# Delta-rule attention with a gated MLP: a new chunk loop in the source's order, with one tile per kind for both sides and two matmul streams in opposite quadrants

## The chip, the core and the metric

The kernel runs on one core of a Trainium2 chip. The time is device time in microseconds (us) of one execution, lower is better. A profiled execution comes with a trace of every engine: PE (TensorE, matmuls), PEld (its weight loads), DVE (VectorE), ACT (ScalarE), POOL (GpSimd) and SP (SyncE, which here only issues DMAs). The span is the time from the first to the last instruction of the trace.

## The reference

Two parts follow each other. The first is a recurrence over 768 tokens for each of 32 heads (4 batches of 8 heads, head dimension 48), with normalized keys:

```python
for t in range(S):
    y[:, :, t] = einsum('bhd,bhde->bhe', q[:, :, t], state)
    v_old = einsum('bhde,bhd->bhe', state, kt)
    state = state + bt * einsum('bhd,bhe->bhde', kt, vt - v_old)
```

The heads' outputs are laid side by side to x, (4, 768, 384). The second part is a gated MLP: h = gelu(x @ w_in) with w_in (384, 1024); the left half of h is u, the right half is normalized over its 512 columns and mixed over the tokens by w_sg (768, 768), plus a bias for each token; the product with u goes through w_out (512, 384) and is added to x.

## The kernel before, in words

**Chunks.** The recurrence is cut into 12 chunks of 64 tokens (NCH = 12, T = 64). Within a chunk it becomes a small triangular system for each head. The 32 heads lie as two sides of 16: side 0 on partitions 0 to 63, side 1 on 64 to 127. Two chunks form a segment (NSEG = 6).

**Triangular part.** `gram` (L174) makes k·kT and k·qT of a chunk: one matmul for each head, 48 rows of contraction, 128 columns (k and q side by side in `kd`). ACT copies the k part to `g`, which goes to DRAM (`gd`); DVE or ACT with POOL masks the q part into `MQ`. `lanes_a` (L223) reads the diagonal 32x32 blocks of a whole segment back as `z`, 128 blocks on 128 partitions, and makes the norms. `lanes_b` (L265) inverts the blocks by elimination on DVE, 30 steps of up to four tensor operations (L282, L286). `zstore` (L295) takes the inverted blocks through DRAM to the two tiles `ZW` of each chunk, one for each side. `solve` (L325) forms the corner block between the two 32x32 blocks with 32x32 matmuls (`corner`, two steps) and then `keys`: key times inverse, into free rows of the same ZW tile.

**Chain.** `chain` (L379) is the part that goes from chunk to chunk: `update` (one matmul for a head over 112 or 128 rows, which hold the value rows and the state rows together), `state` (key times update, added into a bank of PSUM that is never cleared) and `read` (again 112 or 128 rows). `us` holds the scaled values (`vprep`, on POOL, L375) and the state side by side.

**MLP, first half.** `ffn` (L472) takes 128 rows of x for two batches: transposes, a split into a high and a low part for three-term matmuls (`mm3`, L464 to L466), the value half (512 columns) with gelu, moments and the normalization, and four gate blocks (256 columns). x, u and the normalized values go to DRAM. There are 12 such units. Ten are handed out as filling in the chunk loop, the last two follow after it.

**MLP, second half.** After the loop `spatial` and `project` do the token mixing and the last matmul for one batch after another.

**What sets the order.** The loop at L606 weaves lists of steps by their index, `weave` puts the ffn steps between them by a running balance `lack` (L71, L89), `bank` may add filler matmuls on a tile `busy` (L75), and on top of that the program is ordered by a planner that simulates the engines: an instruction is issued where the planner puts it, not where it stands in the source. Two points are fixed by hand (`issue_after`, L588). All large DMAs are issued by SP.

**Precision.** The small matmuls are float32: each one is two MATMUL instructions with a weight load each, so a step over 16 heads is 32 instructions in the trace when both sides go along with 8 heads.

Of the kernel before, what the change touches and what calls it, by code (L numbers as in the profile page):

```python
# [18 lines left out]
DM = NH * HD  # L19
# [14 lines left out]
DIM = (slice(64, 112), slice(0, 48))  # L34
ROWS = (slice(0, 112), slice(0, 128))

DUTY = 1.0
N_KICK = 20  # L40
N_WARM = 9
XB = 2
AHEAD = 500.0
GQ = lambda nc: nc.sync
CREDIT = 2000.0
STREAMS = ((0, 7), (7, 32))
N_SOFT = 6
# [3 lines left out]
def delta_rule_gmlp_kernel(  # L51
    ctx: ExitStack,
    tc: tile.TileContext,
    kqT: bass.AP,
    ktok: bass.AP,
# [9 lines left out]
    nc = tc.nc  # L65

# [4 lines left out]
    lack = [0.0]  # L71

    def keep_warm(ps, n, lhsT=None):
        for _ in range(n):
            nc.tensor.matmul(out=ps, lhsT=busy[:, 0:P] if lhsT is None else lhsT, rhs=busy, start=True, stop=True)  # L75

    def bank(most=0):
        ps = psum.tile([P, 512], F32, name="ps")
        while most > 0 and lack[0] > 0:
            keep_warm(ps, 1)  # L80
            lack[0] += DUTY * 216 - 512
            most -= 1
        return ps

    def mm(out, lhsT, rhs, start=True, stop=True):
        nc.tensor.matmul(out=out, lhsT=lhsT, rhs=rhs, start=start, stop=stop, skip_group_check=True)  # L86
        k, m = lhsT.shape
        n = math.prod(rhs.shape[1:])
        lack[0] += DUTY * (max(0.833 * m, 0.833 * n) + 5) - 2 * n * k / P  # L89
        lack[0] = max(lack[0], -CREDIT)  # L90

    busy = const.tile([P, 512], BF16, name="busy")
    nc.vector.memset(busy, 0.0)
    kick = const.tile([P, P], BF16, name="kick")
    nc.vector.memset(kick, 0.0)

    ident = const.tile([P, P], F32, name="ident")
    make_identity(nc, ident)
    beta_l = const.tile([P, NSEG, 32], F32, name="beta_l")
    nc.scalar.dma_start(out=beta_l, in_=beta)  # L100
    winh = const.tile([P, NC, DFF], F32R, name="winh")
    winl = const.tile([P, NC, DFF], F32R, name="winl")
    xD = [dram.tile([NT, P, DM], F32, name=f"xD{b}", bufs=1) for b in range(NB)]
    vD = [dram.tile([NT, P, DH], F32, name=f"vD{b}", bufs=1) for b in range(NB)]
    uD = [dram.tile([ND, P, SEQ], F32, name=f"uD{b}", bufs=1) for b in range(NB)]
# [8 lines left out]
    N_MQ, N_ZW, N_K, N_US, N_KD, N_G = 6, 3, 3, 2, 4, 5  # L114

    mask = prep.tile([P, T], F32, name="mask")
    nc.gpsimd.memset(mask, 1.0)
    for sd in range(2):
        nc.gpsimd.affine_select(
            out=mask[TOK[sd]], in_=mask[TOK[sd]], pattern=[[1, T]], base=0,  # L120
            channel_multiplier=-1, compare_op=ALU.is_gt, fill=0.0,
        )

    kd = [prep.tile([112, 2, NH, T], F32, name=f"kd{i}") for i in range(N_KD)]

    MQ = [[(low if i < 3 else main).tile([P, NP, T], F32, name=f"mq{sd}_{i}") for i in range(N_MQ)] for sd in range(2)]
    ZW = [[main.tile([P, NP, T], F32, name=f"zw{sd}_{i}") for i in range(N_ZW)] for sd in range(2)]
    US = [[main.tile([P, NP, HD], F32, name=f"us{sd}_{i}") for i in range(N_US)] for sd in range(2)]
    KT = [main.tile([P, NP, HD], F32, name=f"kt{i}") for i in range(N_K)]
    for i in range(N_MQ):  # L130
        nc.gpsimd.memset(MQ[1][i][32:64], 0.0)

    def clear_zw(i):
        nc.gpsimd.memset(ZW[0][i][32:64, :, 0:32], 0.0)
        nc.gpsimd.memset(ZW[1][i][96:128, :, 0:32], 0.0)
        nc.gpsimd.memset(ZW[1][i][32:64], 0.0)

    for i in range(N_ZW - 1):
        clear_zw(i)
    for i in range(N_US):  # L140
        nc.gpsimd.memset(US[1][i][32:64], 0.0)
    nc.gpsimd.memset(US[0][0][64:112], 0.0)
    nc.gpsimd.memset(US[1][0][0:48], 0.0)

    cb = [bank() for _ in range(NB)]
# [13 lines left out]
    G, kqs, gdt, ztile = {}, {}, {}, {}  # L159

    def load(c, hf):
        if c >= NCH:
            return
        kq = kd[(2 * c + hf) % N_KD]
        kqs[c, hf] = kq
        nc.sync.dma_start(out=kq, in_=kqT[c, :, :, hf * NH:hf * NH + NH])

    def qload(c):
        for sd in range(2):
            nc.sync.dma_start(out=MQ[sd][c % N_MQ][DIM[sd]], in_=kqT[c, 64 * sd:64 * sd + HD, 1])  # L170

    def gram(c):
        if c >= NCH:
            return []  # L174
        c2, mqi = c % 2, c % N_MQ
        if c2 == 0:
            gdt[c // 2] = dram.tile([2, 2, 2, NP, 32, 32], F32, name="gd")
        gd = gdt[c // 2]
        g = main.tile([P, NP, T], F32, name="g", bufs=N_G)
        G[c] = g  # L180

        def quad(qd):
            kq = kqs[c, qd // 2]
            ps = bank(3).rearrange("p (j x t) -> p j x t", x=2, t=T)
            for j4 in range(4):
                j = (4 * qd + j4) % NH
                for sd in range(2):
                    rows = slice(64 * sd, 64 * sd + HD)
                    mm(ps[TOK[sd], j4], kq[rows, 0, j], kq[rows, :, j])
                yield  # L190
            js = slice(4 * qd, 4 * qd + 4)
            nc.scalar.copy(out=g[:, js, :], in_=ps[:, :, 0, :])  # L192
            for sd in range(2):
                mq = MQ[sd][mqi][TOK[sd], js, :]
# [578 lines left out]
```

## Time and profile before

| | |
|---|---|
| median of 3 runs | 656.38 us (651.7 to 660.0) |
| the profiled execution | 651.14 us |
| its span | 649.4 us |
| mean granted TensorE clock | 0.841 |
| PE busy | 523.4 us, 81% |
| PEld busy | 454.4 us, 70% |
| DVE busy | 379.8 us, 58% |
| ACT busy | 255.6 us, 39% |
| POOL busy | 135.7 us, 21% |
| DMA queue of SP | 81.95 MB, 47% of the 16 engines' span |

Busy time of PE is the union of the modelled spans of its matmuls, which overlap each other; the rate of a stream of matmuls is read from the distance between starts. The granted clock is 0.50 or 1.00 at any moment; a figure between them is a mean over a stretch. DVE, ACT and POOL execute in the order of their queues, as does SP with its DMA issues: one that waits holds up those behind it.

### The profile page before, as it was taken

To read this page: it belongs to the slowest core of one execution; us is meant where nothing else is said; L and a number is where in the kernel's file an instruction comes from. 1 tells how busy PE (TensorE), PEld (TensorE's weight loads), DVE (VectorE), ACT (ScalarE), POOL (GpSimd) and SP (SyncE) were. 2 spreads that over 40 slices of the span, in tenths; PEclk is the share of its full clock that TensorE was granted. 3 is DMA by queue.
4 is the path that set the end of the run, shared out by engine and by line. 5 is a ranking of instruction groups with operands and counts; after the bars stand their busy time and mean duration, and the time that the engine had idled before them with its cause. 6 is when DMAs were issued, how large, how long until landed. Compare 5 with 4: busy or idle time off the path is not lost. (4 is left out here: it accounts for less than half of the span.)

```text
span 649.4 us, 16992 instructions
## 1 busy us (share of the span) xinstructions
PE 523.4 (81%) x6943; PEld 454.4 (70%) x6943; DVE 379.8 (58%) x1274; ACT 255.6 (39%) x581; POOL 135.7 (21%) x142
## 2 busy tenths in 40 slices
PE   7272794634588696975799979898899999999997
PEld 5251473624467484854678858786789999999997
DVE  3899799119823697349714795396467453533332
ACT  2140372613363454542455646457654121311100
POOL 8326561132001020010101011131001321222210
PEclk9655777557779598987779979599999999999999
DMA  9898540564246364650463334544598264431123
GB/s 205 219 228 190 131 141 26 117 160 126 79 90 156 90 189 126 151 141 25 133 146 100 108 99 132 118 138 125 152 304 262 78 203 122 144 106 51 49 74 111
DMA packets 114175, 86.81 MB, mean 134 GB/s; under 512 B 68272, under 2 KB 96560, under 8 KB 114096
## 3 DMA queue, kind: packets, MB, share of 16 engines
q1 hardware_dynamic: 108864, 81.95, 47.0%
q0 software_dynamic: 864, 3.15, 1.5%
q10 hardware_dynamic: 4368, 0.62, 0.6%
q8 instruction: 55, 0.90, 0.6%
q14 instruction: 24, 0.20, 0.1%
HBM read 56.85 MB, written 28.84 MB: 132 GB/s over the span
## 5 line engine op out<-in xcount | busy, mean ns | idle before, releaser
L375 POOL TENSOR_TENSOR us<-us,nv 64x768 f32<-64x768 f32 x24 | 38.7, 1617 | 233.7 <-DMA us<-vtok 125.5
L86 PE MATMUL ps<-kd 48*64 48x128 f32 x768 | 67.7, 333 | 23.2 <-DMA kd<-kqT 18.0
L282 DVE TENSOR_TENSOR ztmp<-z 128x119 f32<-128x119 f32 (+36 forms) x318 | 77.1, 274 | 1.2
L86 PEld LDWEIGHTS ps<-kd 48*64 48x64 f32 x768 | 55.2, 167 | 31.8 <-DMA kd<-kqT 19.9
L286 DVE TENSOR_TENSOR z<-z,ztmp 128x119 f32<-128x119 f32 (+36 forms) x318 | 73.5, 262 | 1.2
L701 POOL TENSOR_TENSOR ga<-ga,uT 128x384 f32<-128x384 f32 x32 | 33.8, 1055 | 153.8 <-ACT ut L534 51.8
L86 PE MATMUL ps<-us,mq 112*64 112x48 f32 (+1 forms) x768 | 40.1, 242 | 28.7 <-ACT zw L364 13.2
L86 PEld LDWEIGHTS ps<-us,mq 112*64 112x64 f32 (+1 forms) x768 | 36.1, 155 | 36.2 <-ACT zw L364 13.7
L545 ACT CAST gh<-ga 128x384 fp32r<-128x384 f32 x32 | 16.4, 514 | 102.7 <-POOL ga L701 102.6
L464 PE MATMUL ps<-winh,xh 128*128 128x512 f32 x72 | 38.6, 537 | 16.5 <-ACT xh L545 16.5
L202 DVE TENSOR_TENSOR mq<-ps,mask 64x256 f32<-64x256 f32 x64 | 27.0, 421 | 35.3 <-ACT g L192 27.7
L464 PE MATMUL ps<-xh,winh 128*128 128x256 f32 x144 | 42.4, 301 | 1.9 <-DVE mq L202 1.9
L465 PE MATMUL ps<-xl,winh 128*128 128x256 f32 x144 | 40.4, 282 | 0.0
L466 PE MATMUL ps<-xh,winl 128*128 128x256 f32 x144 | 40.3, 282 | 0.0
L546 DVE TENSOR_TENSOR gl<-ga,gh 128x384 fp32r<-128x384 f32 x32 | 17.8, 555 | 38.3 <-ACT gh L545 38.3
L364 ACT COPY zw<-ps 48x512 f32<-48x512 f32 x48 | 27.9, 581 | 27.4 <-PE ps L86 26.8
L86 PE MATMUL ps<-zw,kt 64*48 64x64 f32 x768 | 32.5, 242 | 6.8 <-DVE mq L202 6.4
L86 PE MATMUL ps<-us,zw 128*64 128x48 f32 (+1 forms) x768 | 36.4, 239 | 1.5 <-ACT zw L364 1.2
L466 PE MATMUL ps<-winh,xl 128*128 128x512 f32 x72 | 32.7, 454 | 5.1 <-DVE xl L546 5.1
L86 PEld LDWEIGHTS ps<-zw,kt 64*48 64x48 f32 x768 | 28.0, 139 | 11.9 <-issue 7.1
L86 PEld LDWEIGHTS ps<-us,zw 128*64 128x64 f32 (+1 forms) x768 | 31.7, 151 | 5.8 <-issue 3.6
L86 PEld LDWEIGHTS ps<-j,ztk 32*32 32x32 f32 x768 | 18.4, 127 | 24.8 <-ACT j L350 11.9
(139 smaller groups left out, 1280.4 us busy)
## 6 DMA issues: line engine op xcount, KB each, us to landing
kd<-kqT SPq DMA_DIRECT2D x24, 448.0 KB, 6.1
uD<-ut SPq DMA_DIRECT2D x24, 256.0 KB, 3.6
uT<-uD SPq DMA_DIRECT2D x8, 768.0 KB, 4.8
vD<-vg SPq DMA_DIRECT2D x20, 256.0 KB, 2.9
vraw<-vD SPq DMA_DIRECT2D x20, 256.0 KB, 4.2
us<-vtok SPq DMA_DIRECT2D x24, 192.0 KB, 3.8
kt<-ktok SPq DMA_DIRECT2D x12, 384.0 KB, 3.9
mq<-kqT SPq DMA_DIRECT2D x24, 192.0 KB, 7.5
```

The costliest lines, as they stand in the source:

```text
L86: nc.tensor.matmul(out=out, lhsT=lhsT, rhs=rhs, start=start, stop=stop, skip_group_check=True)
L202: nc.vector.tensor_tensor(out=mq, in0=ps[TOK[sd], :, 1, :], in1=mask[TOK[sd]].unsqueeze(1).broadcast_to([64, 4, T]), op=ALU.mult,)
L282: nc.vector.tensor_tensor(out=tv, in0=z[:, r0:r1, i:i + 1].broadcast_to([P, r1 - r0, w]), in1=z[:, i:i + 1, i + 1:32].broadcast_to([P, r1 ...
L286: nc.vector.tensor_tensor(out=z[:, r0:r1, i + 1:32], in0=z[:, r0:r1, i + 1:32], in1=tv, op=ALU.add)
L364: nc.scalar.copy(out=ZW[sd][zi][DIM[sd], js], in_=ps[DIM[sd]])
L375: nc.gpsimd.tensor_tensor(out=us[TOK[sd]], in0=us[TOK[sd]], in1=nvs[c // 2][TOK[sd], c % 2].unsqueeze(2).broadcast_to([64, NP, HD]), op=AL ...
L464: nc.tensor.matmul(out=ps, lhsT=sh, rhs=mh, start=(first and i == 0), stop=False)
L465: nc.tensor.matmul(out=ps, lhsT=sh, rhs=ml, start=False, stop=False)
L466: nc.tensor.matmul(out=ps, lhsT=sl, rhs=mh, start=False, stop=(last and i == n - 1))
L545: nc.scalar.copy(out=hi, in_=src)
L546: nc.vector.tensor_tensor(out=lo, in0=src, in1=hi.bitcast(F32), op=ALU.subtract)
L701: nc.gpsimd.tensor_tensor(out=ga, in0=ga, in1=uT[:, d], op=ALU.mult)
```

## The change

The whole part between the constants and the second half of the MLP is written anew. The mathematics stays the same.

**Order.** Everything up to the end of the chunk loop stands under `tc.manual_schedule(engines=None)`: all five queues are issued in the order of the source. Only the second half of the MLP is still planned. The fillers on `busy` in `bank`, the balance `lack` and `weave` are gone; the two runs of dummy matmuls before the loop (9 and 20) stay.

**Tiles.** The pairs `MQ[0], MQ[1]`, `ZW[0], ZW[1]` and `US[0], US[1]` become single tiles over 128 partitions: M (masked q part), Z (inverse), W (key times inverse), U (update), V (scaled values), S (state), QO (q with the sides exchanged, from a new array `qsT`). One copy evicts both sides, where there was one for each side. The zero rows and their memsets are gone.

**Matmuls.** A 112- or 128-row matmul of `update` becomes two: `own` (64 rows, the values) and `old` (48 rows, the state), into the same bank; `read` becomes `read` (64 rows) and `ask` (48 rows). `gram` becomes `kgram` and `qgram` with 64 columns each. `deal` issues two lists head by head in turn: one uses the array's diagonal quadrants (rows of a side to columns of the same side), the other the crossed ones.

```diff
-        for sd, j, h, us, out in pairs:                    # update
-            mm(out[TOK[sd], h], ZW[sd][c % N_ZW][ROWS[sd], j], us[ROWS[sd], j])
+    def own(hf):
+        def step(h):
+            if h == 0:
+                ub[hf] = view(bank())
+            for sd in range(2):
+                j = 8 * hf + h
+                ins = mm(ub[hf][TOK[sd], h], z[TOK[sd], j], v[TOK[sd], j], start=(h == 0))
+            if h == 7 and c > 0:
+                ended[hf] = nc.gpsimd.memset(flag, 0.0)
+                wait_for(ended[hf], ins)
+        return step, (lambda: evict_u(hf)) if c == 0 else None
+    def old(hf):
+        def step(h):
+            for sd in range(2):
+                j = 8 * hf + h
+                ins = mm(ub[hf][TOK[sd], h], w[OPP[sd], j], s[OPP[sd], j], start=False)
+                if h == 0 and sd == 0:
+                    wait_for(ins, ended[hf])
+        return step, lambda: evict_u(hf)
...
+    kg, kept = kgram(c + AHEAD), lambda: None
+    if kg:
+        kg[1], kept = (kg[1][0], None), kg[1][1]
...
+        deal([own(0), own(1), *kg, *idle], [ask(0), ask(1), old(0), old(1)])
+        kept()
+    deal([read(0), read(1)], [state(0), state(1)] if c + 1 < NCH else [])
```

**Lanes in portions.** The elimination of a segment is cut into 18 portions (`first` with the norms, `scale`, 15 times two steps, `last`), the decoding of w_in into three portions for each of its six blocks. They stand in one list `bg`; `tick(n)` issues the next n of them at that point of the source.

**The loop.** The chunk's grams run five chunks ahead (AHEAD = 5), the MLP unit two chunks behind, one unit for each chunk with 64 tokens of all four batches, so that there are two iterations more, for the last two units.

```diff
+for c in range(NCH + 2):
+    ffn = Ffn(c - 2) if c >= 2 else None
+    if c + AHEAD + 1 < NCH:
+        kload(c + AHEAD + 1)
+    if c > 0:
+        qload(c + 1); tload(c + 1); vload(c + 1)
+    if ffn:
+        ffn.turn()                       # transposes, split; one tick in it
+    if c < NCH:
+        tick(1); chain(c); gstore(c + AHEAD, (nc.sync,)); tick(3)
+        xstore(c); corner_a(c + 1)
+    if ffn:
+        ffn.value(0); tick(2)
+    if c < NCH:
+        corner_b(c + 1)
+        if c + AHEAD < NCH and (c + AHEAD) % 2 == 1:
+            zload((c + AHEAD) // 2)
+    if ffn:
+        ffn.moments(0); tick(1); ffn.value(1); tick(1); ffn.moments(1); ffn.norm()
+    if c + 1 < NCH:
+        vprep(c + 1); tick(1)
+        deal(qgram(c + AHEAD), keys(c + 1))
+    if ffn:
+        ffn.scale()                      # now on ACT, by the result of norm() on DVE
+    if c % 2 == 0 and c + 2 < NCH:
+        s = (c + 2) // 2
+        while s not in ztile:
+            tick()
+        fetch = zstore(s)                # stores z, and its transpose by an ACT copy
+    if c % 2 == 0 and c + 4 < NCH:
+        new = lanes((c + 4) // 2)
+        bg += new
+    if ffn:
+        ffn.gate(0); ffn.gate(1); tick(1)
+    if fetch:
+        fetch(); fetch = None            # 16 DMAs from DRAM to Z and ztk of two chunks
+    if ffn:
+        ffn.gate(2); ffn.gate(3); tick(1); ffn.ustore()
+    if c == 1:
+        while bg[0] is not new[0]:       # the rest of the decoding of w_in
+            tick()
...
```

Ahead of the loop the k halves of chunks 0 and 1 are loaded first, one by SP and one by ACT; their `g` is stored by both; then `zload(0)`, the q grams, the decoding of one block of w_in, and `lanes(0)`. The grams of chunks 2 to 4 follow, then `zstore(0)`, the corners of chunk 0, and `bg` is filled with `lanes(1)` and the decoding of the other five blocks.

**Other moves.** `vprep` goes from POOL to DVE, the masking of the q part to one DVE operation over 128 partitions and 512 elements, the scaling by the norm in the MLP from DVE to ACT. The corner step uses four 32x32 tiles of the array at a time, where it used two. The stores of x, u and the values are now four for each chunk, of 64 tokens. The decoding and splitting of w_out and w_sg is in portions as well and is issued from chunk 10 on.

943 lines of the change are left out of this document (504 added, 439 removed).

## The prediction

> **What bounds the kernel now.** First I cut the span into stages, by where chunks begin: chunk 3 at 194, chunk 6 at 299, chunk 9 at 401, the last read at 472.4, the last gate's gelu at 499. The columns are length, busy time (instructions) of PE, PEld, DVE, ACT, POOL, granted clock, DMA share, GB/s.
>
> ```profile
> core 0 of [0], span 649.4 us
> 194.00:299.00 105.00, 86.12 (x1533) 70.22 (x1529) 62.64 (x247) 49.40 (x116) 12.08 (x8) 0.85 0.52 136
> 299.00:401.00 102.00, 86.22 (x1496) 70.76 (x1494) 66.25 (x293) 50.65 (x116) 10.25 (x7) 0.83 0.37 102
> 401.00:472.40 71.40, 64.98 (x1079) 54.30 (x1075) 41.08 (x125) 45.03 (x103) 11.01 (x12) 0.90 0.52 144
> 472.40:499.00 26.60, 26.36 (x173) 24.02 (x174) 17.83 (x55) 14.78 (x32) 0.00 (x0) 1.00 0.89 290
> 499.00:649.50 150.50, 146.48 (x840) 146.16 (x838) 62.09 (x107) 23.83 (x45) 33.76 (x32) 0.99 0.35 109
> ```
>
> The end, 150.4 us to the span's end, is matmul after matmul at the full clock, and the change leaves it alone. So the case is decided in the 472 us before. There a chunk costs 34.5 us (chunks 3 to 8) and 23.8 us (9 to 11). PE is busy 82 to 91% of these stretches at a clock of 0.83 to 0.90; DVE only 58 to 65%. The stretch is set by PE: its work, its clock, and 15 to 19 us of idleness in each three chunks.
>
> Second, the rates of PE's steps, from starts in the order of time at the full clock (start, length, instruction):
>
> ```profile
> 275.09 1.14 PE L86 MATMUL ps<-us,zw 112*64 112x48 f32 x32
> 276.16 0.69 PE L86 MATMUL ps<-zw,g 32*32 32x32 f32 x32
> 276.78 0.55 PE L491 MATMUL ps<-ident,x 128*128 128x128 f32 x3
> 277.26 1.09 PE L86 MATMUL ps<-kd 48*64 48x128 f32 x16
> 278.28 0.55 PE L491 MATMUL ps<-ident,x 128*128 128x128 f32 x3
> 278.76 0.92 PE L86 MATMUL ps<-us,kt 64*48 64x48 f32 x32
> 279.61 0.50 PE L464 MATMUL ps<-winh,xh 128*128 128x512 f32 x1
> 279.95 0.40 PE L465 MATMUL ps<-winl,xh 128*128 128x512 f32 x1
> 280.18 0.39 PE L466 MATMUL ps<-winh,xl 128*128 128x512 f32 x1
> ```
>
> ```profile
> 366.48 1.10 PE L86 MATMUL ps<-zw,kt 64*48 64x64 f32 x32
> 367.51 0.39 PE L464 MATMUL ps<-xh,winh 128*128 128x256 f32 x1
> 367.74 0.28 PE L465 MATMUL ps<-xl,winh 128*128 128x256 f32 x1
> 367.85 0.28 PE L466 MATMUL ps<-xh,winl 128*128 128x256 f32 x1
> ```
>
> From start to next start: an update of 32 instructions 1.07 us, a corner step 0.62, a gram quarter 1.02, a state step 0.85, keys 1.03, three transposes 0.48, a 512-column matmul 0.23 (0.34 the first), a 256-column one 0.11 (0.23 the first).
>
> Third, whether two streams in opposite quadrants run beside each other. Keys (crossed) and half a gram (diagonal) are already interleaved once a chunk; the same 0.90 us, first the instructions on the tile kt, then those on kd:
>
> ```profile
> 229.13:230.03 0.90, 0.89 (x32) 0.90 (x32) 1.00 0.00 0
> ```
>
> ```profile
> 229.13:230.03 0.90, 0.87 (x16) 0.76 (x18) 1.00 0.00 0
> ```
>
> 32 instructions of keys (1.03 alone) and 16 of gram (1.02 alone) took 0.90 together: the cost is the larger, not the sum.
>
> **PE, part by part.** Per chunk and at the full clock, before: two update and two read halves, 4 x 1.07 = 4.3; state 2 x 0.85 = 1.7; gram 4 x 1.02 = 4.1, which covers keys; corners 4 x 0.62 = 2.5. Together 12.6. After: own and kgram beside ask and old is 2 x 0.85 + 2 x 1.03 = 3.8 against 3.4, so 3.8 (a 64-column gram is priced as keys, the own, old, ask halves as state); read beside state 1.7; qgram beside keys 2.1; corners 2.5 at most, half of that if four tiles overlap. Together 8.9 to 10.1, I take 10.1, as no row shows the four. The MLP unit is 2 x 0.48 + 18 x 0.23 + 36 x 0.11, and about 0.12 more at each of six first matmuls: 9.8, as before. So PE's chunk goes from 22.4 to 19.9: three quarters of the expected overlap only pays for splitting the tall matmuls in two.
>
> The Trainium skill (TensorE: Matmul & The Clock Gate, Part 3, What overlaps and what doesn't) says that a weight load overlaps matmuls in flight only in another group of rows. Both streams use both row groups, so by that rule they would add up; the two rows of 0.90 us disagree.
>
> **DVE.** It gains a role, as every portion stands at a fixed point between PE's steps.
>
> ```profile
> 150.40:174.70 24.30, 21.06 (x106) 0.74 0.44 115
> ```
>
> ```profile
> 214.13 0.18 DVE L150 TENSOR_SCALAR rsq_y<-d 128x32 int32<-128x32 int32 x1 [11.82 <-ACT d L231]
> ...
> 219.99 0.19 DVE L242 SCALAR_TENSOR_TENSOR nb<-nb,beta_l 128x32 f32<-128x32 f32 x1
> 220.28 1.22 DVE L269 TENSOR_TENSOR z<-z,nb 128x1024 f32<-128x1024 f32 x1
> ```
>
> ```profile
> L512 DVE BATCH_NORM_STATS2 bs<-vg 128x6 f32<-128x512 f32 x20 | 13.8, 692 | 23.9 <-ACT vg L510 23.7
> L718 DVE TENSOR_TENSOR o<-ps,x 128x384 f32<-128x384 f32 x24 | 13.3, 556 | 29.4 <-PE ps L466 21.0 <-DMA out<-o 8.4
> L546 DVE TENSOR_TENSOR xl<-ps,xh 128x384 fp32r<-128x384 f32 x24 | 13.3, 554 | 33.8 <-ACT xh L545 33.5
> ```
>
> The first row is DVE on ztmp alone, the 106 operations of a segment's elimination: 21.1. The norms take 6.1 (214.13 to 220.2) less about 1.2 of other work in between, 4.9; the two scalings 1.22 each. A segment is 28.5, call it 29. The rest of a chunk: two xl 1.1, two moments (0.69 and about 0.2) 1.8, the MLP norm (11 small operations in a row; the 15 of the norms above took 4.9, or 0.33 each with one long one among them, so about 0.27) 2.9, the two masks (0.55 x 512/384 each) 1.5, vprep (1.22 x 768/1024) 0.9: 8.2. By the ticks, chunk 2 issues a whole segment, 37; odd chunks 3, 5, 7 twelve portions, mostly steps, 16.9 + 8.2 = 25; even chunks some 19.
>
> **Waits added.** `old` waits for a POOL memset behind `own`: `own(1)` beside `ask(1)`, 0.85 us, covers it, unless POOL holds one of its long operations (below, 2.91), so 0 to 2.9 in a chunk with decoding or a new segment. ACT's `scale` waits for the norm on DVE and holds back the gates' gelus, and the transposing copy in `zstore` waits for a segment's end with the same queue behind it; PE then lacks banks. In chunks 3 to 8 this ties PE to DVE. ACT itself, busy 49.4 of 105 above, loses as many evictions as it gains scalings, and I cost it at nothing. SP gets about 29 issues a chunk at 0.51 (below): 15 us, under the chunk's time.
>
> **The start.** It is ordered by arrival of `z`, DVE, and the way through DRAM:
>
> ```profile
> 25.85 0.25 ACT L231 COPY d<-z 128x32 f32<-128x32 f32 x1 [1.19 <-DMA z<-gd]
> ```
>
> ```profile
> 64.83 0.34 SPq L302 DMA_DIRECT2D zd<-z  x1
> ...
> 73.20 0.68 DVE L440 TENSOR_TENSOR vg<-vg,winh 128x512 f32<-128x512 f32 x1
> 73.36 2.91 POOL L439 TENSOR_TENSOR ut<-ut,vg 128x512 f32<-128x512 f32 x1 [3.40 <-DVE ut L436]
> 73.44 1.02 SPq L312 DMA_DIRECT2D zw<-zd  x2
> ...
> 73.56 0.22 PE L86 MATMUL ps<-zw,g 32*32 32x32 f32 x2 [4.51 <-DMA zw<-zd]
> ```
>
> `z` at 22 (four earlier by smaller first loads and two queues; 18 to 26); segment 0 done at 51; through DRAM 8.8 (64.83 to 73.56), 60. Chunk 0's PE work with the corners of chunk 1, 12.6 at half clock as PE has been idle, 25, and 4 for evictions: 89. Then DVE, which waited for qgram(5)'s mask, has 13 portions of segment 1 left, 18 + 1.5: 109. DRAM 9, corners and qgram 12 at half clock: 130. Ten decode portions, two thirds of five blocks of seven operations at 0.42 to 0.68 (4.2 each): 144. Chunk 2: 37, 5 for an MLP unit at half clock, 4 for the held gelus: 190. Bounds 178 and 205; before it was 194, so nothing is won here.
>
> **The sum.** Chunks 3 to 8: the floor is 22.5 (DVE 25 in odd chunks, PE 19.9 in even ones); the ceiling is 19.9 at the same clock of 0.84 and the same 17% of idleness, 28.5. I take 27, nearer the row, since the queues stay coupled: 6 x 27 = 162 (before 207). Chunks 9 to 11: no grams, 19.5 / 0.90, and 0.6 for a wait: 22.3 each, 67 (71.4). Two last units: 12 each, 9.8 and the way from transpose to xl, 24 (26.6). End 150.4. Together 190 + 162 + 67 + 24 + 150.4 = 593.4; the profiled execution lasts 651.14 - 649.4 = 1.7 longer, 595; the median is 656.38 / 651.14 = 1.008 of it: **600 us**.
>
> **The rivals.** A: DVE and PE come to the floors, corners half the price, `z` early: 178 + 135 + 63 + 24 + 150.4 + 1.7, times 1.008, 557; chance 0.10. B: source order costs what the planner's did, chunks stay at 34.5 and 23.8: 190 + 207 + 71 + 27 + 152, 652; for it speaks that PE idled 17% even with a planner, against it that DVE had room; 0.10. C: the streams add up after all, by the rule above: 3.4 + 1.7 + 2.1 = 7.2 more a chunk, 8.5 at the clock, in nine chunks 76 less some 18 that DVE covers: 658; 0.04. D, slower: the fillers are gone and the clock stays at half.
>
> ```profile
> 118.50:132.20 13.70, 13.22 (x282) 0.50 0.73 146
> ```
>
> Here PE alone is shown, 97% busy for 13.7 us with small matmuls, and the clock stayed at 0.50. PE's chunk is then 39.8, nine of them 358, the last units 40: 190 + 358 + 40 + 152 = 740, 746. It decides from a mean clock of 0.64 down (nine chunks at 31.7). Against it: every chunk holds 8 us of full-array matmuls, and with as many the rows show 0.83 to 0.90. Chance 0.11. The Trainium skill (the same page, Part 1, What's actually happening) has a busy window of about 3.4 us lift the clock, by which D could hardly happen; this row disagrees, so I keep D's chance.
>
> **Chances and range.** The forecast holds 0.65. About 2% is what a measurement tells from no change, 643 to 669. Faster: the forecast, A and a little of B, 0.76; within: most of B and C, 0.13; slower: D, 0.11. The range goes from 548 (A and a bit) to 655 (B); it leaves out D and C.
>
> **What would show it.** Right: `own` and `ask` starting within one 0.9 us stretch; chunk 3 near 190; DVE nearly full from 22 to chunk 8, with PE's idleness ended by ACT or DVE; clock near 0.85; 27 and 22 us a chunk; 150 us at the end. Wrong: chunks above 30 us, a clock below 0.7, PE waiting for POOL's memset or for Z from DRAM, or a start that reaches far beyond 205.

## The result and the profile after

The changed kernel takes 678.84 us in the median (676.86 to 681.13, 4 runs) against 655.17 us of the kernel before on the same chip (651.7 to 660.0, 4 runs): 1.036 times as long, 95% interval 1.028 to 1.043. It is slower; 600 us was predicted. Some executions run over 1.5% longer than the fastest of their kernel; the ratios here leave those out, the medians do not, and the profiled execution of `e13_gates` below (597.72 us) is one of them.

First the stages, by the same view as before: chunk 3's chain starts at 214.4, chunk 9's at 402.8, the last read ends at 474.9, the last gate's matmul at 521.5. Columns: length, busy time (instructions) of PE, PEld, DVE, ACT, POOL, granted clock, DMA share, GB/s.

```profile
0.00:214.40 214.40, 95.54 (x2658) 83.35 (x2658) 127.02 (x473) 45.50 (x91) 22.59 (x38) 0.67 0.49 121
214.40:402.80 188.40, 142.05 (x3949) 126.44 (x3949) 113.75 (x491) 73.62 (x162) 3.59 (x14) 0.78 0.56 136
402.80:474.90 72.10, 54.84 (x1401) 49.89 (x1401) 29.87 (x102) 25.69 (x61) 5.26 (x14) 0.80 0.55 142
474.90:521.50 46.60, 31.95 (x178) 27.55 (x177) 22.79 (x71) 19.12 (x42) 0.00 (x0) 0.79 0.53 153
521.50:675.20 153.70, 149.83 (x864) 149.50 (x862) 65.29 (x107) 29.44 (x57) 34.47 (x32) 1.00 0.43 134
```

| stage, us | before | predicted | after |
|---|---|---|---|
| to chunk 3's chain | 194 | 190 | 214.4 |
| chunks 3 to 8 | 207 | 162 | 188.4 |
| chunks 9 to 11 | 71.4 | 67 | 72.1 |
| to the last gate | 26.6 | 24 | 46.6 |
| the end | 150.4 | 150.4 | 153.7 |
| span | 649.4 | 593.4 | 675.1 |

Against the kernel before, the middle won 19 us, and the start and the tail lost 20 each. PE's busy time fell from 523.4 to 474.2 us, and the span still grew: PE is now idle for 201 us (675.1 - 474.2) where it was idle for 126. The matmul work was saved. It was not what set the time.

Who waits for whom is in the view of waits, here some of its rows (engine, line and tile that waited <- what ended it: us in total, times, longest):

```profile
PE ps L71 <- issue: 39.4, 23, 8.3
...
DVE v L415 <- DMA v<-vtok: 35.1, 6, 14.6
PE ps L71 <- DMA kd<-kqT: 33.0, 5, 10.6
PE ps L71 <- DMA kt<-ktok: 31.8, 4, 14.7
...
PE ps L315 <- DVE n L267: 27.6, 1, 27.6
...
PE ps L71 <- POOL flag L443: 10.1, 2, 6.7
```

Three of these rows are loads from DRAM (`v`, `kd`, `kt`), 100 us of waiting between them, on DVE and PE; these waits overlap, so they are not 100 us of the span. None of the three stood in the prediction. ("issue" marks stands that the view cannot put down to anything; the longest, 8.3 us, ends 8 us after the issue of the `kt` that its matmul reads and looks like one more wait for it. The others are taken up in the last section.) SP's issues around chunk 8 tell why (start, us, queue, line, copy, count):

```profile
344.54 0.53 SPq L332 DMA_DIRECT2D zd<-zl  x1
345.17 0.45 SPq L334 DMA_DIRECT2D ztd<-zt  x1
347.94 2.82 SPq L342 DMA_DIRECT2D z<-zd  x4
350.87 2.87 SPq L350 DMA_DIRECT2D ztk<-ztd  x4
353.83 1.99 SPq L342 DMA_DIRECT2D z<-zd  x4
355.92 3.19 SPq L350 DMA_DIRECT2D ztk<-ztd  x4
359.20 2.10 SPq L645 DMA_DIRECT2D uD<-ut  x4
361.36 0.53 SPq L124 DMA_DIRECT2D qo<-qsT  x1
361.94 0.43 SPq L128 DMA_DIRECT2D kt<-ktok  x1
362.41 0.43 SPq L132 DMA_DIRECT2D v<-vtok  x1
```

The loads of the next chunk stand behind the whole round trip of the inverses: two stores, 16 fetches that wait for them, and the stores of u. They are issued 17 us after `zd`: 13.9 us of that are the 22 issues themselves, 2.3 the wait for `zd` to land. Ahead of these rows the queue had stood for 11.8 us at the stores of `vg`, which wait for ACT. What SP waited for in the whole run, by the same view:

```profile
SPq L213 <- ACT g L198: 90.6, 9, 33.4
SPq L631 <- ACT vg L628: 87.8, 12, 11.8
...
SPq L342 <- DMA zd<-zl: 9.4, 6, 2.4
```

So the landing of `zd` is the small part (9.4 us); the stores of g and of the values, which wait for ACT, are the large one. Over chunks 3 to 8 SP's 164 issues take 110.6 of the 188.4 us. The queue has room; it is in the wrong order.

### The profile page after: what moved, and what is told of

The parts are those of the page before. It is cut to its first block, busy times and chain, and to the rows that moved or that the text cites. A ratio compares the mean times of both kernels' runs of the same rounds, so it can differ in the third digit from the quotient of the medians.

```text
span 675.1 us, 20911 instructions
## 1 busy us (share of the span) xinstructions
PE 474.2 (70%) x9043; PEld 436.7 (65%) x9043; DVE 358.7 (53%) x1243; ACT 193.4 (29%) x410; POOL 65.9 (10%) x98
## 5 line engine op out<-in xcount | busy, mean ns | idle before, releaser
L71 PE MATMUL ps<-kd 48*64 48x64 f32 x1536 | 70.6, 267 | 57.4 <-DMA kd<-kqT 33.0
L293 DVE TENSOR_TENSOR zl<-zl,ztmp 128x119 f32<-128x119 f32 (+36 forms) x318 | 69.5, 252 | 1.4
L289 DVE TENSOR_TENSOR ztmp<-zl 128x119 f32<-128x119 f32 (+36 forms) x318 | 69.3, 252 | 1.4
L71 PE MATMUL ps<-z,kt 64*64 64x64 f32 x704 | 34.2, 269 | 40.5 <-DMA kt<-ktok 31.8
L71 PEld LDWEIGHTS ps<-z,kt 64*64 64x64 f32 x704 | 31.9, 181 | 43.0 <-issue 42.2
L870 POOL TENSOR_TENSOR ga<-ga,uT 128x384 f32<-128x384 f32 x32 | 34.5, 1082 | 153.7 <-DVE ga L868 103.6
L71 PE MATMUL ps<-u,mq 64*64 64x48 f32 x768 | 37.0, 268 | 8.5 <-issue 8.4
L71 PE MATMUL ps<-v,z 64*64 64x48 f32 x768 | 31.9, 246 | 12.5 <-ACT ut L640 12.1
L71 PEld LDWEIGHTS ps<-v,z 64*64 64x64 f32 x768 | 29.9, 161 | 15.3 <-ACT ut L640 13.2
L71 PEld LDWEIGHTS ps<-u,mq 64*64 64x64 f32 x768 | 35.0, 186 | 6.1 <-issue 5.7
L71 PE MATMUL ps<-s,w 48*64 48x48 f32 x704 | 29.6, 248 | 12.3 <-POOL flag L443 10.1
L71 PEld LDWEIGHTS ps<-s,w 48*64 48x64 f32 x704 | 27.8, 164 | 14.4 <-POOL flag L443 10.4
```

The lines of the kernel that those rows point to most:

```text
L71: return nc.tensor.matmul(out=out, lhsT=lhsT, rhs=rhs, start=start, stop=stop, skip_group_check=True)
L289: nc.vector.tensor_tensor(out=tv, in0=z[:, r0:r1, i:i + 1].broadcast_to([P, r1 - r0, w]), in1=z[:, i:i + 1, i + 1:32].broadcast_to([P, r1 ...
L293: nc.vector.tensor_tensor(out=z[:, r0:r1, i + 1:32], in0=z[:, r0:r1, i + 1:32], in1=tv, op=ALU.add)
L870: nc.gpsimd.tensor_tensor(out=ga, in0=ga, in1=uT[:, d], op=ALU.mult)
```

## The experiments

Every ratio below is to the kernel before on the same chip. The runs came in four sets on different chips, in which the kernel before had medians of 650.47 (1 to 4), 654.42 (5), 655.61 (6 and 7) and 653.85 (8), so a difference of a few us between two sets says little, and the difference of the two ratios is the safer figure; within a set medians can be compared.

**1. The loads one chunk earlier.** `e1_loads` issues the loads of q, kt and v right after the chain of the chunk before, and the next k behind its q grams, so that none stands behind the round trip.

```diff
     if c < NCH:
         tick(1); chain(c)
+        qload(c + 2); tload(c + 2); vload(c + 2)
         gstore(c + AHEAD, (nc.sync,))
...
-    if c > 0:
-        qload(c + 1); tload(c + 1); vload(c + 1)
```

> The loads of k, q and v for a chunk are issued ahead of the z round trip on SP instead of behind it: q, k by token and v of chunk c+2 right after chain(c), kd of chunk c+7 right after qgram(c+5). Nothing is left out. Theory SP (in the source's order the loads stand behind 18 DMAs that wait for a segment's end): PE's waits for kd before kgram(5) (6.9 us) and for kt or v before keys(2), keys(4), keys(6), keys(8), keys(10) (14.7, 6.4, 8.3, 6.0, 4.7 us) go, DVE no longer stands 14.6 us before vprep(2), and chunk 3 starts near 195 instead of 214; 635 to 650 us in all. Rival (DVE and ACT in order set the pace; the loads only happen to be late): another wait takes their place, 665 to 678 us.

Measured 635.96 us, 0.980 [0.974, 0.985]: 43 us less than the changed kernel (37 by the two ratios, (1.036 - 0.980) x 655; 42 by the two spans), by moving some lines. Some of its waits, and its stages:

```profile
PE ps L315 <- DVE n L267: 25.1, 1, 25.1
...
PE ps L71 <- POOL flag L443: 12.2, 2, 8.7
...
DVE v L415 <- DMA v<-vtok: 1.7, 1, 1.7
```

```profile
0.00:207.30 207.30, 101.97 (x2660) 89.15 (x2660) 127.10 (x473) 45.71 (x91) 22.59 (x38) 0.68 0.53 136
207.30:365.80 158.50, 130.92 (x3947) 116.10 (x3947) 113.25 (x491) 73.25 (x162) 3.59 (x14) 0.90 0.63 156
365.80:432.00 66.20, 50.41 (x1401) 45.95 (x1401) 29.78 (x102) 25.42 (x61) 5.25 (x14) 0.85 0.54 140
432.00:479.40 47.40, 33.87 (x176) 28.91 (x177) 22.69 (x71) 18.95 (x42) 0.00 (x0) 0.77 0.50 144
```

The wait for `v` falls from 35.1 to 1.7, the one for `kt` is gone; `kd` keeps 22.4, all of it ahead of the loop. Chunks 3 to 8 now take 158.5 us, 26.4 each, and chunks 9 to 11 66.2: the prediction's 27 and 22.3. What remains is the start (207.3, where 195 was expected) and the tail, which the loads hardly touch.

**2. The weights of the tail earlier.** `e2_w`, on the changed kernel, begins the decoding of w_out and w_sg one chunk earlier.

```diff
-        if c == NCH - 3:
+        if c == NCH - 4:
```

> The decoding and splitting of w_out and w_sg starts one chunk earlier (from chunk 9 on). Nothing is left out. Theory W (its DMA waits stand in the queues of ACT and DVE between the steps of the last MLP units): the stretch from the last read to the last gate falls from 46 us to 30 to 36, chunks 9 to 11 grow by 5 at most; 664 to 671 us. Rival (the unit's own round from transpose to scaling sets the tail): the stretch stays above 42 us; 674 to 680 us.

Measured 675.21 us, 1.039 [1.035, 1.044]. The tail became shorter (519.0 less 479.3, 39.7), and chunks 9 to 11 became longer by as much (399.8 to 479.3, 79.5 instead of 72.1). The work was only pushed ahead. Neither expectation holds whole: the tail lies between the two, the time is the rival's.

**3. The planner again.** `e3_planner` is the changed kernel without the order by hand.

```diff
-    by_hand.enter_context(tc.manual_schedule(engines=None))
```

> The line with manual_schedule is taken out, so that the planner orders the new loop as it did the old one; tiles, matmuls and streams stay. Theory order (the new tiles and streams save PE time, the source's order loses it again): 590 to 635 us. Rival (the new tiles save nothing, or the planner cannot use them): 645 us or more. A third reading, that order does not matter, gives 670 to 685.

Measured 670.31 us, 1.031 [1.024, 1.037]. By medians that is 8 us less than the changed kernel, by the ratios 3, and the two intervals overlap: no difference is shown. With the planner the new loop is as slow, so source order as such isn't the loss.

**4. The streams one after the other.** `e4_seq`: `deal` issues the first list whole, then the second.

```diff
-        for i in range(max(len(d), len(x))):
-            for r in (d, x):
-                if i < len(r) and r[i]:
...
+        for r in (d, x):
+            for s, done in r:
...
```

> deal issues the whole diagonal list and then the whole crossed one, so that the two streams follow each other. Nothing is left out. If the streams overlap as the rows of before showed, PE has 3.4 + 1.7 + 2.1 = 7.2 us more in a chunk at full clock, some 9 at the granted one, of which the stalls hide a part: 30 to 80 us more, 705 to 755. If they did not overlap in the changed kernel: within 5 us of 678.

Measured 671.83 us (one run), span 670.1, that is 7 us less than the changed kernel (2 by the ratio of 1.033 to its own chip's median), not 26 or more above it. The first expectation missed; the second, within 5 us, is missed by 1 us or met, according to which figure is taken, and its condition, that the streams do not overlap, is refuted by what follows. The reason isn't that the streams fail to overlap. Here are the instructions of `own` (tile `v`) of chunk 4, first of the changed kernel, where `ask` runs between them, then of `e4_seq`, where nothing does:

```profile
246.90:249.10 2.20, 2.07 (x64) 1.95 (x64) 0.00 (x0) 1.00 0.67 151
```

```profile
246.90:249.20 2.30, 2.07 (x64) 1.94 (x64) 0.00 (x0) 1.00 0.69 158
```

64 instructions take 2.07 us in both, so `ask` rides along for nothing. But over chunks 3 to 8 of `e4_seq`:

```profile
209.60:395.80 186.20, 160.09 (x3949) 148.31 (x3949) 113.55 (x491) 74.97 (x162) 3.59 (x14) 0.89 0.58 138
```

PE is busy for 160.1 us of 186.2 at a clock of 0.89; in the changed kernel for 142.1 of 188.4 at 0.78. The 18 us of busy PE that the interleaving saves came back whole as idle time, and with a lower granted clock beside it.

**5. Three waits that remain.** Each edit is made on `e1_loads`. `e6_norms` takes the first portion of `lanes(2)` and the transpose that waits for it ahead of the decoding of w_in, which chunk 1 works off:

```diff
         if c == 1:
-            while bg[0] is not new[0]:
+            bg.remove(new[0]); new[0](); norms(2)
+            while bg[0] is not new[1]:
                 tick()
```

> The kernel of e1_loads (636.0 us), and in chunk 1 the first step of the third segment's lane work and its row scale (the transpose that TensorE waits for) are issued ahead of the seven decodings of w_in, not behind them. My theory: of e1_loads' idle stretch 138.2 to 163.3 (25.1 us, ended by VectorE's n) all but a few us is TensorE waiting in order for a tile that VectorE reaches only after the decodings. Chunk 2's chain then starts at 142 to 148 instead of 164.8, and runs beside the decodings; the first MLP unit must still wait for them, so chunk 3's chain comes at 192 to 199 instead of 207.3, and the time is 621 to 628 us. Rival: the decoded weights themselves are what is late; then chunk 2's chain starts early, TensorE idles behind it instead, chunk 3 stays at 205 to 209, and the time at 633 to 638.

Measured 630.85 us, 0.967 [0.962, 0.971], between the two. Chunk 2's chain starts at 139.8 instead of 164.8, but chunk 3's only at 197.3. The wait for `n` falls from 25.1 to 4.5, and another takes its place:

```profile
PE ps L71 <- DVE xl L598: 26.3, 4, 19.8
```

PE now stands 19.8 us for the first unit's `xl`, which is behind the same decoding on DVE. The chain was 25 us early and could use 10.

`e7_tail` issues, for the last three units, the gates right behind the values, and moments, norm and scale behind the next unit's transposes.

```diff
-        ffn.moments(0); tick(1); ffn.value(1); tick(1); ffn.moments(1); ffn.norm()
...
-        ffn.scale()
+    if held: finish(held)      # behind the next turn(): moments, norm, scale
```

> The kernel of e1_loads (636.0 us), and for the last three MLP units the source order is changed: the gates of a unit come right behind its second value matmuls, and its moments, norm and scale are issued behind the transposes of the next unit. My theory: the tail (last read to last gate, 47.4 us in e1_loads) is long because source order makes each unit a serial round, in which the next unit's copies on ScalarE stand behind a scale that waits for VectorE's norm; without that the three idle stretches of 6.7, 2.4 and 4.4 us go, the tail is 33 to 38, and the time 623 to 629 us. Rival: the splits of w_sg, whose raw tiles arrive late, hold ScalarE and VectorE in order; then the tail stays above 43 and the time at 632 to 637.

Measured 629.39 us, 0.965 [0.960, 0.971]. The tail is 42.6 instead of 47.4 (last read to the last gate's matmul): 5 us, less than the expected 9 to 14. Why, the next step shows.

`e8_sub` moves the decoding's subtraction from POOL to DVE, so that POOL's flag has nothing ahead of it.

```diff
-            nc.gpsimd.tensor_tensor(out=lowf, in0=lowf, in1=mf, op=ALU.subtract)
+            nc.vector.tensor_tensor(out=lowf, in0=lowf, in1=mf, op=ALU.subtract)
```

> The kernel of e1_loads (636.0 us), and the subtraction of the weights' decoding, the only work of GpSimd in the late chunks beside the flag, is done by VectorE. My theory: the idle stretches of TensorE before the matmuls that wait for GpSimd's flag (8.7 and 3.4 us in chunks 10 and 11 of e1_loads) come from the flag's memset standing in order behind a subtraction that waits for a transfer; they go to under 1 us each, and the time is 624 to 629 us. Rival: the stretch is the wait for the decoding's transfers by another engine too (VectorE or ScalarE stand in order behind the same transfer), and only its name changes: 633 to 638.

Measured 628.22 us, 0.962 [0.954, 0.970]. No wait for POOL's flag is left on PE, and chunks 9 to 11 take 58.4 instead of 66.2.

`e9_all` has the three together.

> The three edits of e6_norms, e7_tail and e8_sub together on e1_loads (636.0 us). If the three waits are independent the savings add up, 10 + 11 + 9 us by the middle of what each is expected to give, and the time is 598 to 615 us, 6 to 8% under the kernel before. Rival: each wait covers another (the late transfers, the lower clock with denser work), and the three together give less than half of that: 622 or more.

Measured 623.94 us, 0.956 [0.950, 0.962]: 12 us less than `e1_loads`, where the three alone gave 5.1, 6.6 and 7.7 by the same reckoning (by ratios, 16 against 9, 9 and 11). So they do not add up, and both halves of the kernel had to be looked at again. At the start, this row of DVE in `e9_all` stands out (start, us, operation, in brackets the idle time before it):

```profile
100.50 0.69 DVE L233 TENSOR_TENSOR mq<-ps,mask 128x512 f32<-128x512 f32 x1 [25.57 <-PE ps L71]
```

DVE stands for 25.6 us at a mask that waits for PE, and behind it in the queue is `lanes(1)`, whose data have long been there. In the tail ACT stands three times for over 3 us for transfers, twice for raw tiles of w_sg and once for the values read back for the second half, with the next unit's copies behind it:

```profile
430.69 0.62 ACT L576 CAST vnh<-vraw 128x512 fp32r<-128x512 f32 x1 [3.84 <-DMA vraw<-vD]
...
442.25 0.51 ACT L576 CAST wsgh<-raw 128x384 fp32r<-128x384 f32 x1 [3.75 <-DMA raw<-w_sgT]
...
456.59 0.51 ACT L576 CAST wsgh<-raw 128x384 fp32r<-128x384 f32 x1 [3.94 <-DMA raw<-w_sgT]
```

**6. The lane work in one piece; the weights on another queue.** `e10_lanes`, on `e9_all`:

```diff
-    bg += lanes(1)
+    for part in lanes(1):
+        part()
```

> The kernel of e9_all (623.9 us), and the whole of the second segment's lane work is issued before chunk 0, where e9_all hands it out in small parts through chunk 0. In e9_all VectorE stands from 74.9 to 100.5 (25.6 us) at a mask multiply that waits for TensorE, with 26 of the 30 steps of this lane work queued behind it. My theory: this stand is what makes chunk 2's inverses late (stored at 120.6) and then the decodings of w_in, that is, what is left of the long start; the lane work then ends at 88 to 92, the decodings at 145 to 150 instead of 163, chunk 3's chain starts at 178 to 186 instead of 197.7, and the time is 604 to 612 us. Rival: the decodings are held by the loads of w_in and of the chunks on the transfers' side, and chunk 3 stays later than 192: 618 to 624.

Measured 599.85 us, 0.923 [0.907, 0.939]: 24 us less than `e9_all` (21 by the ratios), more than expected. Chunk 3's chain starts at 175.8 instead of 197.7. In its view of waits DVE's standing at the masks has shrunk, from 48.2 us in `e9_all` (25.6 the longest) to this:

```profile
DVE mq L233 <- PE ps L71: 25.9, 9, 12.1
```

`e11_wq`, on `e9_all`, loads the raw tiles of w_out and w_sg by POOL's queue and three ahead instead of two:

```diff
-                    nc.sync.dma_start(
+                    nc.gpsimd.dma_start(
```

> The kernel of e9_all (623.9 us), and the raw tiles of w_out and w_sg are loaded by GpSimd's queue, three ahead, not by SyncE's, two ahead. My theory: in e9_all's tail (last read 424.7 to last gate 470.6, 45.9 us) ScalarE stands in order at the splits of w_sg, whose raw tiles are issued behind the stores and the reloads of the end on SyncE (stands of 3.8, 3.8 and 3.9 us), and the copies of the next unit's transposes stand behind them; from another queue they come in time, the tail is 34 to 40 and the time 612 to 619 us. Rival: the units' own round of TensorE, ScalarE and VectorE sets the tail: 43 or more, 621 to 626.

Measured 616.51 us, 0.950 [0.939, 0.960]: the tail is 39.1 us instead of 45.9.

`e12_both` has both.

> The edits of e10_lanes and e11_wq together on e9_all (623.9 us). They lie in different stages, so their savings should add up: 592 to 603 us. If either is covered by something else, 604 to 616.

Measured 592.24 us, 0.912 [0.900, 0.924]. Its stages:

```profile
0.00:172.50 172.50, 98.62 (x2657) 86.37 (x2658) 130.26 (x479) 45.19 (x91) 13.34 (x32) 0.69 0.63 163
172.50:333.80 161.30, 131.17 (x3947) 116.40 (x3947) 113.13 (x491) 73.45 (x162) 3.59 (x14) 0.88 0.62 153
...
393.00:434.30 41.30, 31.76 (x177) 27.18 (x176) 20.73 (x59) 19.53 (x44) 4.81 (x9) 0.81 0.60 174
```

**7. The old loop in source order.** `e5_before_hand` is the kernel before with one addition, and with its two points fixed by hand taken out:

```diff
+    by_hand.enter_context(tc.manual_schedule(engines=None))
```

> The kernel before with its old chunk loop, every queue in the order of its source, as the changed kernel has it, and nothing else changed. If source order were itself the loss of the changed kernel, this is slower than before by about as much or more: 670 to 720 us. If the loss belongs to the new loop (where its loads, its lane work and its tail stand), the old loop loses little: 645 to 665. By the changed kernel's prediction source order cost nothing, which is the second.

Measured 791.96 us, 1.220 [1.208, 1.232], beyond both ranges, on the side of the first. The old source was written for a planner and its order had never counted, so this run says what that order is worth, not what source order costs the new loop. In its view of waits a load leads again:

```profile
POOL us L377 <- DMA us<-vtok: 357.6, 12, 56.5
```

**8. Four runs at the end.** `e13_gates`, on `e12_both`, issues all four gates of an even chunk ahead of ACT's copy of the inverses. In `e12_both` ACT stands at that copy, and PE behind the gates' Gelus, which wait their turn (ACT's row, then PE's first row of chunk 3):

```profile
170.26 1.95 ACT L333 COPY zt<-zl 64x1024 f32<-64x1024 f32 x1 [10.71 <-DVE zl L304]
```

```profile
172.54 0.45 PE L71 MATMUL ps<-v,z 64*64 64x48 f32 x4 [10.41 <-ACT ut L640]
```

```diff
+        if ffn:
+            for d in range(4): ffn.gate(d)     # with their ticks
         if c % 2 == 0 and c + 2 < NCH:
             ...
             fetch = zstore(s)
```

> The kernel of e12_both (592.2 us), and in each even chunk the copy of the inverses on ScalarE (with their stores) is issued behind the gates of the MLP unit, not ahead of them. In e12_both ScalarE stands 10.7 us at that copy before chunk 3 (159.5 to 170.3, until VectorE has ended the lane work), the gates' Gelus stand behind it, and TensorE stands 10.4 us for their banks. My theory: that stand goes, chunk 3's chain starts at 162 to 166 instead of 172.5, and the time is 580 to 586 us. Rival: the inverses of chunk 4, which now leave some us later, or VectorE's lane work itself are what counts; then chunk 4's chain is no earlier than in e12_both (201.1) and the time is 590 to 596.

Measured 589.46 us, 0.901 [0.894, 0.907]; the intervals of this and of `e12_both` overlap, so a gain isn't shown, and the time lies just under the rival's range. The chunks are read from `e14_seq`, which has the same order of the gates. There chunk 3's chain starts at 162.6, 10 us earlier than in `e12_both` (172.5), but chunk 4's at 202.5, no earlier than 201.1. The stand has moved into chunk 3:

```profile
174.33 0.56 PE L71 MATMUL ps<-s,qo 48*64 48x48 f32 x6 [7.76 <-ACT g L196]
```

ACT's copy still waits for DVE's lane work, and now it is the eviction of a gram (`g`) that stands behind it and PE that lacks its bank. For the chunks the rival was right.

`e14_seq` is `e13_gates` with the deal of `e4_seq`.

> The kernel of e13_gates with the two streams dealt out one after the other, not alternately, so that the tiles of one quadrant follow each other. In the changed kernel itself this cost 36 us of busy TensorE and no time. My theory: there the saved work had only become idle time, because loads and lane work set the pace; with those stands gone the middle chunks are bounded by TensorE again, and the sequential deal is slower than e13_gates by 12 to 36 us. Rival: TensorE's work in the small matmuls is not what bounds any stage, or the granted clock rises to meet the denser work: within 6 us of e13_gates.

Measured 592.60 us, 0.906 [0.900, 0.912], 3 us from `e13_gates` and inside the rival's 6. The five chunks 4 to 8, first of `e12_both` (interleaved, its gates behind ACT's copy), then of `e14_seq`:

```profile
201.10:333.80 132.70, 108.13 (x3247) 95.76 (x3246) 86.30 (x372) 60.95 (x132) 3.41 (x12) 0.88 0.61 154
```

```profile
202.50:337.40 134.90, 124.37 (x3249) 113.50 (x3248) 90.73 (x396) 61.54 (x135) 3.42 (x12) 0.96 0.58 145
```

Interleaving saves 16.2 us of busy PE here and gains 2.2 us of time; the idle time grows from 10.5 to 24.6, and the clock falls from 0.96 to 0.88.

`e15_planner` is `e13_gates` under the planner.

> The kernel of e13_gates with the planner in charge of the order again, as in the kernel before. In the changed kernel the planner in place of source order gave 670 instead of 679 us. My theory: the source's order was the worse only where single instructions stood at the wrong place, and these are mended now, so the planner gives no less than source order: 595 to 660 us. Rival: the planner's freedom is worth its 8 us or more here too: 572 to 585.

Measured 666.47 us, 1.021 [1.014, 1.027], 77 us more than the same program in source order and above both ranges. On a source whose order is wrong in places the planner was as good as source order, on the mended one it is 77 us worse; it stays near 670 with either.

`e16_late_loads` is `e13_gates` with the loads back behind the round trip.

> The kernel of e13_gates with the loads of k, q and v back where the changed kernel has them, one chunk later, behind the round trip of the inverses on SyncE's queue. On the changed kernel this one edit was worth 43 us (678.8 to 636.0). If its worth does not depend on the other edits, this is 38 to 48 us slower than e13_gates; if the two overlap (the late loads also delayed what the other edits now bring early), 10 to 37.

Measured 630.64 us, 0.965 [0.959, 0.971]: 41 us more, where the same edit was worth 43 on the changed kernel. The cost of the loads stands by itself.

## Why the prediction was wrong

The predicted 600 us lie 79 us under the result. The chain of edits is worth as much: the loads 43 (678.8 to 636.0), the norms, the tail and the subtraction 12 together (to 623.9), the lane work in one piece 24 (to 599.9), the weights' queue another 8 (to 592.2); by the ratios 37, 16, 21 and 7. None of them touches a matmul of the chunk loop or its tiles. That `e12_both` ends near the forecast is in part luck: its chunks 3 to 8 take the forecast time (161.3 for 162), but its start is 17 us shorter than forecast, its chunks 9 to 11 are 8 shorter and its tail is 17 longer.

**The step that failed first: SP.** The prediction has "SP gets about 29 issues a chunk at 0.51 (below): 15 us, under the chunk's time". The size is near: in chunks 3 to 8 a chunk has 27 issues at 0.67, 18 us. The step that failed is that it priced the queue by its load and put its order at nothing. What costs is the order: the loads stand behind stores that wait for ACT (90.6 and 87.8 us in the rows above) and behind the 22 issues of the round trip. With the loads moved, these two waits of SP still come to 53.0 and 49.9 us in `e1_loads`, but the loads of q, kt and v are issued almost a chunk sooner. Two runs put the order at 43 and 41 us.

**The start** was forecast at 190 and came at 214.4. Step by step, with DVE's and SP's rows of the changed kernel:

```profile
45.37 0.37 SPq L120 DMA_DIRECT2D kd<-kqT  x1
59.02 2.55 SPq L213 DMA_DIRECT2D gd<-g  x4
61.68 0.44 SPq L332 DMA_DIRECT2D zd<-zl  x1
```

```profile
48.99 1.23 DVE L304 TENSOR_TENSOR zl<-zl,nb 128x1024 f32<-128x1024 f32 x1
...
116.31 1.23 DVE L304 TENSOR_TENSOR zl<-zl,nb 128x1024 f32<-128x1024 f32 x1
...
144.56 0.96 DVE L415 TENSOR_TENSOR v<-v,nv 128x768 f32<-128x768 f32 x1 [14.59 <-DMA v<-vtok]
...
170.47 0.69 DVE L533 SCALAR_TENSOR_TENSOR winl<-ut,vg 128x512 fp32r<-128x512 f32 x1 [1.18 <-POOL ut L529]
```

Segment 0 was done on DVE at 50.2, as forecast (51), but SP stored it at 61.7: its store stands behind those of chunk 4's gram, which wait for a load of k issued at 45.4 (PE stands 10.6 us for it). That is SP's order once more, 11 us that the forecast did not have; no run moved it alone. Segment 1 was done at 117.5, not 109; the decodings at 171, not 144. The prediction saw that DVE stands at qgram(5)'s mask with segment 1 behind it, and took it as given. It is the largest term of the start: `e10_lanes` removed it and won 22 us there. For the decodings it added DVE's operations and no wait; the 14.6 us for `v`, a load behind the round trip, and those for the raw tiles and for POOL came on top.

**Chunks 3 to 8** were forecast at 162 and took 188.4; with the loads alone mended they take 158.5. The size was right. The reason was not: "The stretch is set by PE: its work, its clock, and 15 to 19 us of idleness". The streams do overlap as the prediction's two rows of 0.90 us said. Two halves of `own` beside `ask` took 2.07 us against its 1.7, and PE's busy time in these chunks came out lower than without the interleaving, 142 against 160. Yet time and saved work are not the same thing: in `e4_seq` and `e14_seq` PE does 16 to 18 us more and the kernel takes as long. The idle share of 17% that the prediction took over from before came out with the loads mended (27.6 of 158.5 us in `e1_loads`), but by luck: 18.5 of the 27.6 us are stands of the kind "issue", at which PE waits for its own instructions (last section), and the kernel before has 0.3 us of them in its whole span. The gain against the kernel before must come from elsewhere in the new loop; which part of it, the single copies for both sides, the order, or the work that changed its engine, wasn't tried one by one.

The Trainium skill (TensorE: Matmul & The Clock Gate, Part 3, What overlaps and what doesn't) lets a weight load overlap only in another group of rows. Both streams use both groups, and the 2.07 us with and without `ask` disagree with it, as the two rows in the prediction did. Rival C, built on it, is out: its 658 us was nearer the result by chance.

**The tail** was forecast at 24 and took 46.6. The term was mis-sized from the start: it counts "two last units". The kernel before has 173 PE instructions in its tail, the changed one 178, and a unit has 60 (6 transposes, 18 and 36 matmuls), so three units lie behind the last read in both. PE's busy time there is 32 us at a clock of 0.79. The other 15 us are a source order that leaves each unit a serial round, and ACT at the raw tiles; `e7_tail` took 5 off, `e11_wq` 7, but they do not add up: with both edits in it `e12_both` still takes 41.3 us with PE busy for 31.8, so some 9 us stay open.

**Waits added.** The prediction let `old`'s wait for POOL's memset cost 0 to 2.9 us in a chunk. It cost 10.1 us in two stands on the changed kernel (6.7 the longest), and 12.2 in `e1_loads`. POOL stood behind a subtraction that waited for its transfer, and a wait isn't bounded by the 2.91 us that the operation takes. The gates' Gelus held behind ACT's copy in `zstore` it named, and put at 4 us; `e12_both` shows 10.4.

**The rivals.** D (the clock stays at half) did not come: the mean clock is 0.80, 0.78 in chunks 3 to 8. What it warned of came in small: the clock is lower where PE has more idle time, 0.78 against 0.90 with the loads mended. B had source order cost what the planner's did; its 652 was for unchanged chunks, and the changed kernel's middle was faster than that. The slower side came by a mechanism that was not on the list: a load or a store behind an issue that waits in one queue, and filling work handed out behind an operation that waits. The list of what would show the prediction wrong had "a start that reaches far beyond 205" and "chunks above 30 us", and both came (214.4; 188.4/6 = 31.4), as did the wait for POOL's memset.

**The end** was right: 153.7 for 150.4.

## What to carry to other kernels

When a program goes from a planner to source order, go through each queue once and ask of every instruction that waits what stands behind it: a prefetch behind stores that wait and a round trip, filling work behind an operation of the critical engine, or a flag behind an operation that waits for a load cost 43, 24 and 8 us here, and none shows in a sum of durations. Busy time saved on an engine is worth time only down to the next limit: in chunks 4 to 8 of `e14_seq` PE works or waits for its own instructions in 134.7 of 134.9 us, and still 16 us less matmul time brought 2. Compare the order with the planner only after the source has been put in order: the planner made no clear difference on the changed kernel and cost 77 us on the mended one.

## What was not expected of the hardware

The granted clock moved against the saved work. In the pair above (`e12_both` and `e14_seq`) it was 0.88 with 108 us of busy PE and 0.96 with 124 in nearly the same time. Whether the lower clock follows from the idle time or from the interleaved matmuls themselves isn't told apart by these runs.

PE also stands without anything that the view of waits can name. First of `e12_both`, then of `e14_seq`:

```profile
PE ps L71 <- issue: 33.1, 24, 4.1
```

```profile
PE ps L71 <- issue: 18.2, 14, 3.3
```

With the interleaved deal there are 24 such stands, 33.1 us; with the sequential one 14, 18.2 us. In chunks 4 to 8 alone it is 16.1 us against 10.3, so 5.8 of the 14.1 us by which the idle time grows there; waits for `xl` on DVE (5.2) and for the Gelus on ACT (2.0) make up most of the rest.

The DMA packets in the same traces tell what PE waits for. One queue, which the page calls "instruction", moves packets of 16,384 bytes each (packets, MB, share of the DMA engines; first the kernel before, then `e12_both`):

```profile
q8 instruction: 55, 0.90, 0.6%
```

```profile
q8 instruction: 71, 1.16, 0.8%
```

Their number goes with PE's instructions: 55 for twice 6,943 matmuls and weight loads, 71 for twice 9,043, so one for 252 to 255. And the stands follow them. Counted in matmuls and weight loads, 22 of the 24 stands of `e12_both` (32.3 us) and 13 of the 14 of `e14_seq` (17.8 us) fall on the same place of a period of 256, give or take one, and each of these ends 1.2 to 1.6 us after such a packet has ended. So PE stands there for its next 256 instructions; the stand of 4.04 us at the state step of chunk 4 in `e1_loads`, `e7_tail` and `e10_lanes` is of this kind too.

It also fits the two deals. In the rows of `own` above, the alternating deal takes 256 instructions (64 matmuls of `own`, 64 of `ask`, a weight load for each) in 2.07 us, the sequential one 128. In the traces of `e12_both` and `e14_seq` no two of these packets start less than 3.4 us apart. So where the deal alternates, PE uses its instructions up faster than they were ever seen to arrive, and where the streams follow each other it doesn't. Splitting the tall matmuls in two, which raised their number from 6,943 to 9,043, made that nearer. All this is read from traces; no edit tested it.
